# U's products clear their bank with a product of zeros, and batch 1's first stage is placed behind layer 1's first products

## The chip, the cores and the metric

The kernel runs on one core of one Trainium2 chip. The metric is the device time of one execution in microseconds; a kernel's time is the median of its runs.

## What is computed

The reference, cut to what matters (x is 8 batches of 3136 rows by 256 columns; all values are float32):

```python
def _attn_ref(x, w_r, w_i, b_r, b_i):
    X = np.fft.rfft(x, axis=1)
    Yr = X.real @ w_r - X.imag @ w_i + b_r
    Yi = X.real @ w_i + X.imag @ w_r + b_i
    lam = 0.01
    Yr = np.sign(Yr) * np.maximum(np.abs(Yr) - lam, 0.0)
    Yi = np.sign(Yi) * np.maximum(np.abs(Yi) - lam, 0.0)
    return np.fft.irfft(Yr + 1j * Yi, n=x.shape[1], axis=1)

def _moe_ref(x, U, V, w_ch1, w_ch2):
    xt = x.transpose(0, 2, 1)
    h = xt @ U @ V                     # U: 3136 x 32, V: 32 x 3136
    u = x + h.transpose(0, 2, 1)
    ch = np.maximum(u @ w_ch1, 0.0) @ w_ch2      # 256 -> 1024 -> 256
    return u + ch
```

The output is the second function applied to the first.

## The kernel before

Each batch goes through two transforms and then two dense layers. The transform of 3136 points is split into one of 49 and one of 64 points. The stages carry the names of their PSUM tiles (a PSUM tile fills one bank of 512 floats per partition):

- `psa` (`a_mm`): the first stage of the forward transform, eight groups c = 0 to 7 a batch. One group is 24 matmuls; ScalarE (ACT) copies one bank out, VectorE (DVE) makes a sum and a difference of the two (into the tiles `xt`), and four transfers, issued by SyncE (SP), store them to memory (`gd`).
- `psb`, `psy`, `psc`: the second forward stage, the product with the complex weights and the shrinking, and the first inverse stage. Batch 0's results go through 32 x 32 transposes on DVE (`zz` from `t0t`).
- `psd` (`d_unit`): the second inverse stage. Its right operand `du` has 81 columns for each frequency: 49 for output points, and 32 more that hold the transform's matrix times U, so that the same matmul gives the projection on U. The stage has six units of two halves each. Every half fills two banks, which ACT copies into `xq` and from which DVE adds 32 columns into `pa`.
- `psu` (`make_ud`): once in the program, the matmuls that fill these 32 columns of `du`, for six groups of frequencies (6, 6, 4, 6, 6 and 4 of them). Each frequency takes four small matmuls, into four bands of partitions of one bank (25, 24, 25 and 24 rows). ACT then copies the four bands out, one operation each, so a group takes four copies, 24 in all. The two banks (`psm0`, `psm1`) that the six groups take in turn also serve the first pair of `psd`.
- `p_spread`, `p_unit`: `pa` is spread by DVE into `pr`, turned by TensorE (`psp`) and written into the tile `w1x`.
- `u_prep`: `psv`, the product with V, is added to `xq` by DVE; from the sum come the operands `oa`, `ob` and `od` (high and low parts, `oah`, `oal` and so on).
- `psy`, `psx`, `psz` and then `pso`: layer 1 in seven half-sized products for each pair of chunks, and layer 2. The tiles `s`, `v`, `rh` and `rl` lie between the two.
- Weights arrive as 64-bit words and are decoded on DVE and ACT (`dm`, `dp`, `dl`, `wa`, `w2t`, `w1x`).
- `setup_w` computes `wt` and `wis`, from which ACT and GpSimd (POOL) make the mixing weights `wmt` of the batches from 1 on.

The program is recorded as a list of operations and ordered by a planner, `_Program.order`, with an estimated cost of each. It runs list passes forward and backward over the operations and their dependences. In the code as written, the place of an operation decides how early it is wanted and who gets a free buffer first. Where TensorE would be idle in the plan, the planner puts fills at line 561: products of an identity, 128 columns each, into a bank that is free (`idle<-ident`); a fill leaves two records in the trace. Nearly all other operations are issued from line 563, so the profile's rows say L563 and are told apart by their tiles.

Batch 0's whole transform comes first. Batch 1's first stage is loaded from line 1648 on. Its groups 0 and 1 are called at line 1658, and groups 2 to 7 on a side list (line 2000) that runs along with the first dense chunks, with positions 2 + 2(c - 2).

Of the kernel before, what the change touches and what calls it, by code (L numbers as in the profile page):

```python
# [29 lines left out]
R = 32  # L30
# [14 lines left out]
K1 = 49  # L45
KP = 56
C81 = K1 + R
# [524 lines left out]
def fft_mix_moe_kernel(  # L572
# [58 lines left out]
    def acopy(o, i):  # L631
        return act.activation(o, i, AF.Copy)
# [137 lines left out]
    def a_mm(b, c, loads=()):  # L770
        xt = a_state.pop((b, c))
        ps = banks(0, f"psa_{b}_{c}")

        def products():

            def mm(j, q, e, o, l, r):
                pe.matmul(
                    ps[j][32 * q : 32 * q + 32, o : o + r.ids[0].size],
                    lhsT=fq[64 * j : 64 * j + K1, l : l + 32],
                    rhs=r,  # L780
                    start=True,
                    stop=True,
                    tile_position=(64 * j, 32 * q),
                    skip_group_check=True,
                )

            for i in range(2):
                for q in range(4):
                    cc, e = divmod(q, 2)
                    if i == 0:  # L790
                        mm(0, q, e, 0, 32 * cc, xt[e][0:K1])
                    own = 64 if (c, e, i) == (0, 0, 0) else 0
                    mm(1, q, e, D * i, own + 32 * cc, xt[1 - e][64 : 64 + K1, 1 - i])

        first = in_group(products)
        first.preds.update((e.n, e) for e in loads)
        p0, p1 = [p.rearrange("p (i d) -> p i d", i=2) for p in ps]
        even, odd = xt
        acopy(odd, p1)
        dve.tensor_tensor(out=even, in0=p0, in1=odd, op=ALU.add)  # L800
        if c == 0:
            for cc in range(2):
                q = slice(64 * cc, 64 * cc + 32)
                acopy(even[q, 0], p0[q, 0])
            lo = odd[:, 1]
            dve.tensor_tensor(out=lo, in0=p0[:, 1], in1=lo, op=ALU.subtract)
            for cc in range(2):
                q = slice(64 * cc + 32, 64 * cc + 64)
                dve.tensor_tensor(out=odd[q, 0], in0=p0[q, 0], in1=odd[q, 0], op=ALU.subtract)
        else:  # L810
            dve.tensor_tensor(out=odd, in0=p0, in1=odd, op=ALU.subtract)
        g = gd[b % 2].rearrange("e k a (s c i) d -> c s a (e k) (i d)", s=2, i=2)
        for cc in range(2):
            at = slice(64 * cc, 64 * cc + 64)
            dma.dma_start(g[c, 0, cc], even[at])
            dma.dma_start(g[c, 1, 1 - cc], odd[at])
# [662 lines left out]
    def load_fdt(c):  # L1479
        dma.dma_start(fdt[:, 8 * c : 8 * c + 8], c_fdt[:, 8 * c : 8 * c + 8, :])  # L1480

    def make_ud(t):
        n0, n = UNITS_D[t]
        ps = psm([128, 512], f"psu_{t}", 2)
        parts = [(64 * j + 32 * r, K1 * j + 25 * r, 25 - r) for j in range(2) for r in range(2)]
        for k in range(n):
            for p, c, m in parts:
                mm = pe.matmul(
                    ps[p : p + m, R * k : R * k + R],
                    lhsT=fdt[:, n0 + k, c : c + m],  # L1490
                    rhs=us[:, n0 + k, :],
                    start=k == 0,
                    stop=k == n - 1,
                    tile_position=(0, p),
                    skip_group_check=True,
                )
                if t > 0:
                    mm.preds[prog.idlers[2].n] = prog.idlers[2]
        for p, _, m in parts:
            p = slice(p, p + m)  # L1500
            u = du[t][p, 0 : n * C81].rearrange("p (q c) -> p q c", c=2 * C81)
            acopy(u[:, :, K1 : K1 + 2 * R], ps[p, 0 : R * n].rearrange("p (q r) -> p q r", r=2 * R))

    def load_v(c):
        load_words(vw[:, 392 * c : 392 * c + 392], (128, 392), ("v", c, 0))
# [103 lines left out]
    def on(n, f, *args):  # L1609
        first.append((n, lambda: f(*args)))  # L1610
# [35 lines left out]
    loads = []  # L1646
# [8 lines left out]

    for c in range(4):
        on(129 + c / 10, load, c)
    on(133, lambda: [a_mm(1, c, loads if c == 0 else ()) for c in range(2)])
    loads1 = []
    for c in range(4):  # L1660
        on(129.5 + c / 10, load, 4 + c, loads1)
# [308 lines left out]
    n = len(prog.ops)  # L1970
# [5 lines left out]
    side = []  # L1976
# [9 lines left out]
    for w, prev, next_w in zip(turn_w, [None] + turn_w, turn_w[1:] + [None]):  # L1986
        b, j = divmod(w, NW)
        if j == 0 and b < NB:
            assert not side
            side = [(6.5, lambda b=b: rest_unit(b))]  # L1990
            if b + 1 < NB:
                start, mid, end = (1, 58, 84) if b else (START, 71, 86)

                side += bmc_spread(b + 1, start, mid - 6)
                if b + 2 < NB:
                    at = four_at(b + 1, start, mid - 6)
                    some = (0, 1, 1, 2, 3, 3, 4, 5) if shared(b + 1) else (0, 1, 2, 2, 3, 4, 4, 5)
                    side += a_spread(b + 2, [at[k] for k in some])
                if b == 0:
                    side += [(2 + 2.0 * (c - 2), lambda c=c: a_mm(1, c, loads1 if c == 4 else loads if c == 0 else ())) for c in range(2, 8)]  # L2000
                    side += [(8 + t, lambda t=t: keep_du(t)) for t in (3, 4, 0, 1, 2)]
                    side += [(32, lambda: dma.dma_start(vd[2:4], vd[0:2]))]
                    side += [(34 + k, lambda k=k: pad_z(1 - k)) for k in range(2)]
                side += d_spread(b + 1, mid - 4, end)
                side += [(end + 0.5, lambda b=b: p_spread(b + 1)), (end + 1.5, lambda b=b: p_unit(b + 1))]
            else:
                side += [(40, rest_load)]
            side.sort(key=lambda z: z[0])
        for g in range(2):
            l1s = l1_chunks(w, g)  # L2010
            new = l2_chunks(w, g)
            for k in range(4):
                for c in range(2):
                    n = WS * j + 8 * g + 2 * k + c
                    if c == 0:
                        l1s[k]()
                    elif l2s:
                        l2s.pop(0)()
                    s = 8 * g + 2 * k + c
                    if s == 1 and next_w not in (LAST, None):  # L2020
                        v_load(next_w)
                    if s == 9 and prev is not None:
                        out_unit(prev)
                    if next_w is not None:
                        if s == 9:
                            up = u_prep(next_w)
                        if s >= 10:
                            up[s - 10]()
                    while side and side[0][0] <= n:
                        side.pop(0)[1]()  # L2030
            l2s = new
# [119 lines left out]
```

## Time and profile before

| what | us |
|---|---|
| median of 3 runs | 1577.74 (1576.67 to 1577.82) |
| profiled execution | 1575.85 |
| its span, first to last instruction | 1574.1 |
| TensorE matmuls (PE) busy | 1546.7 |
| VectorE (DVE) busy | 1294.2 |
| ScalarE (ACT) busy | 926.1 |
| GpSimd (POOL) busy | 421.4 |

PE and PEld are TensorE's matmuls and its weight loads, which run beside the matmuls. "issue" in the chain of waits is time in which an engine waited for nothing that the profile shows. The granted clock (PEclk) is a share of full speed: 1.00 is 2.4 GHz and 0.50 is 1.2 GHz. The queue called "instruction" in the table of transfers carries the engines' own instructions.

### The profile page before, as it was taken

The page shows a single profiled execution, that of the slowest core. Times are in us where ns is not written, and L with a number is a line of the kernel's source. Part 1 is how long each engine was busy: PE and PEld are TensorE (multiplying, and loading weights), DVE is VectorE, ACT ScalarE, POOL GpSimd, SP SyncE. Part 2 cuts the span into 40 slices and gives each one's busy share as a digit, 9 for nine tenths or more (in the row PEclk, how much of TensorE's full clock was granted, in tenths as well). Part 3 has the DMA queues.
Part 4 walks back from the last instruction along what each step waited for, and adds up shares of the span by engine and source line. Part 5 has one row for each costly group of instructions (what it writes and reads, how often), then busy time and mean ns, then how long its engine had stood idle before and what let it go on. Part 6 is the DMA issues. An engine that isn't in the chain of part 4 may idle for free.

```text
span 1574.1 us, 43271 instructions
## 1 busy us (share of the span) xinstructions
PE 1546.7 (98%) x17604; PEld 1392.4 (88%) x17604; DVE 1294.2 (82%) x2351; ACT 926.1 (59%) x1756; POOL 421.4 (27%) x366
## 2 busy tenths in 40 slices
PE   9978999999999999999999999999999999999998
PEld 6966889988898899998898889989898998999997
DVE  5979899689977899779986899778996789866775
ACT  3876565556655666556655666555665565555553
POOL 1311233123322333213331233222232133312221
PEclk9999999999999999999999999999999999999999
DMA  6665566636764465535665465644565025520332
GB/s 159 181 164 126 157 197 160 162 101 160 185 155 112 111 177 135 145 87 143 153 149 137 121 165 134 151 112 112 143 161 144 25 85 123 120 81 8 83 65 37
DMA packets 227309, 201.64 MB, mean 128 GB/s; under 512 B 131127, under 2 KB 191018, under 8 KB 227030
## 3 DMA queue, kind: packets, MB, share of 16 engines
q1 hardware_dynamic: 224472, 198.01, 49.7%
q8 instruction: 139, 2.28, 0.6%
q10 hardware_dynamic: 2638, 0.86, 0.3%
q14 instruction: 60, 0.49, 0.1%
HBM read 118.54 MB, written 82.27 MB: 128 GB/s over the span
## 4 chain that ended last, share of the span: by engine, by line
PE 91%; DVE 4%; DMA 1%; issue 1%; ACT 1%; SPq 1%; POOL 0%; DVEq 0%; POOLq 0%; ACTq 0%
PE pso L563 32%; PE psy L563 18%; PE psx L563 8%; PE psq L563 7%; PE psd L563 6%; PE psa L563 4%; PE psz L563 4%; PE psc L563 4%; PE pst L563 3%; PE psb L563 3%; PE psv L563 1%; PE idle L561 1%; SPq L563 1%; DMA xx<-in_x_dram 1%; DVE ys L563 1%
## 5 line engine op out<-in xcount | busy, mean ns | idle before, releaser
L563 PE MATMUL pso<-rh,w2t 128*128 128x512 f32 x1568 | 407.1, 382 | 0.5 <-issue 0.5
L563 PEld LDWEIGHTS pso<-rh,w2t 128*128 128x128 f32 x1568 | 273.4, 190 | 32.8 <-issue 4.8
L563 PE MATMUL pso<-rl,w2t 128*128 128x512 f32 x784 | 233.6, 379 | 0.4 <-DVE rl L563 0.4
L563 POOL TENSOR_TENSOR yl<-ys,yh 128x512 fp32r<-128x512 f32 x88 | 114.0, 1295 | 250.9 <-ACT yh L563 155.7
L563 ACT ACTIVATE rh<-s 128x512 fp32r<-128x512 f32 x196 | 121.8, 627 | 86.1 <-DVE s L563 81.2
L563 PEld LDWEIGHTS pso<-rl,w2t 128*128 128x128 f32 x784 | 148.0, 189 | 21.9 <-DVE rl L563 1.0
L563 DVE SCALAR_TENSOR_TENSOR rl<-s,rh 128x512 fp32r<-128x512 f32 x196 | 151.5, 777 | 17.1 <-ACT rh L563 15.2
L563 DVE SCALAR_TENSOR_TENSOR ys<-tb,rl 64x256 f32<-64x256 f32 x350 | 156.0, 446 | 9.5 <-ACT rl L563 4.1
L563 PE MATMUL psy<-odh,w1x 128*128 128x256 f32 x784 | 122.1, 278 | 0.9 <-DVE s L563 0.9
L563 PE MATMUL psq<-wmt,xsh 128*128 128x256 f32 (+1 forms) x704 | 122.5, 275 | 0.0
L563 PEld LDWEIGHTS psy<-odh,w1x 128*128 128x128 f32 x784 | 110.7, 192 | 10.3 <-DVE s L563 1.1
L563 POOL TENSOR_TENSOR w1x<-xq,w1x 128x256 fp32r<-128x256 f32 x48 | 35.9, 747 | 299.9 <-DVE tt L563 110.3
L563 PEld LDWEIGHTS psq<-wmt,xsh 128*128 128x128 f32 (+1 forms) x704 | 109.6, 191 | 3.0 <-DVE s L563 0.4
L563 POOL TENSOR_TENSOR tl<-ts,th 128x512 fp32r<-128x512 f32 (+2 forms) x46 | 56.6, 1231 | 183.0 <-ACT th L563 124.3
L563 POOL TENSOR_TENSOR odl<-tt,odh 128x512 fp32r<-128x512 f32 x49 | 63.7, 1301 | 154.5 <-ACT odh L563 92.4
L563 ACT ACTIVATE xq<-psd 128x294 f32<-128x294 f32 (+1 forms) x192 | 69.9, 444 | 52.9 <-PE psd L563 51.8
L563 PE MATMUL psq<-wmt,xsl 128*128 128x256 f32 (+1 forms) x352 | 96.8, 275 | 0.0
L563 DVE SCALAR_TENSOR_TENSOR rl<-psy,rh 128x512 fp32r<-128x512 f32 x98 | 66.9, 683 | 30.7 <-ACT rh L563 29.9
L563 ACT ACTIVATE rl<-tb,lam 128x512 f32<-128x512 f32 x88 | 63.6, 723 | 46.8 <-DVE tb L563 46.5
L563 ACT ACTIVATE s<-psy 128x512 f32<-128x512 f32 x98 | 58.5, 597 | 53.1 <-PE psy L563 49.3
L563 ACT ACTIVATE s<-psx 128x512 f32<-128x512 f32 x98 | 58.2, 594 | 53.4 <-PE psx L563 52.1
L563 ACT ACTIVATE rh<-v 128x512 fp32r<-128x512 f32 x98 | 61.6, 628 | 47.1 <-DVE v L563 46.4
(211 smaller groups left out, 3891.0 us busy)
## 6 DMA issues: line engine op xcount, KB each, us to landing
gd<-xt SPq DMA_DIRECT2D x224, 128.0 KB
zt<-zd SPq DMA_DIRECT2D x112, 224.0 KB
out_dram<-os SPq DMA_DIRECT2D x190, 128.0 KB
t<-gd SPq DMA_DIRECT2D x168, 128.0 KB
zd<-zs SPq DMA_DIRECT2D x84, 256.0 KB
xt<-in_x_dram SPq DMA_DIRECT2D x88, 224.0 KB
vw<-vd SPq DMA_DIRECT2D x44, 256.0 KB
fb<-in_fb_dram SPq DMA_DIRECT2D x54, 128.0 KB
```

The source lines that it names most:

```text
L561: engines["pe"].matmul(o[:, 0:128], lhsT=junk, rhs=junk, start=True, stop=True)
L563: made = call(*[real(a) for a in op.args], **{k: real(a) for k, a in op.kw.items()})
```

## The change

The six groups of `psu` get one more matmul each, ahead of the others: a 128 x 128 block of zeros times 128 or 192 columns of zeros, which starts the bank (`start=True`) on all 128 partitions. The small matmuls then all add to it. With the whole bank written, ACT copies all 128 partitions in one operation. The zeros are the second half of `wt`, which holds them until `setup_w` writes it. At line 1658 no group of batch 1's first stage is called any more; the side list has all eight, at positions 3 + 2c.

```diff
+    zero = wt[:, 1]
+
     def make_ud(t):
...
+        pe.matmul(
+            ps[:, 0 : R * n], lhsT=zero[:, 0:128], rhs=zero[:, 0 : R * n], start=True, stop=False, skip_group_check=True
+        )
         for k in range(n):
             for p, c, m in parts:
                 mm = pe.matmul(
...
-                    start=k == 0,
+                    start=False,
...
-        for p, _, m in parts:
-            p = slice(p, p + m)
-            u = du[t][p, 0 : n * C81].rearrange("p (q c) -> p q c", c=2 * C81)
-            acopy(u[:, :, K1 : K1 + 2 * R], ps[p, 0 : R * n].rearrange("p (q r) -> p q r", r=2 * R))
+        u = du[t][:, 0 : n * C81].rearrange("p (q c) -> p q c", c=2 * C81)
+        acopy(u[:, :, K1 : K1 + 2 * R], ps[:, 0 : R * n].rearrange("p (q r) -> p q r", r=2 * R))
...
-    on(133, lambda: [a_mm(1, c, loads if c == 0 else ()) for c in range(2)])
+    on(133, lambda: [a_mm(1, c, loads if c == 0 else ()) for c in range(0)])
...
-                    side += [(2 + 2.0 * (c - 2), lambda c=c: a_mm(1, c, loads1 if c == 4 else loads if c == 0 else ())) for c in range(2, 8)]
+                    side += [(3 + 2 * (c - 0), lambda c=c: a_mm(1, c, loads1 if c == 4 else loads if c == 0 else ())) for c in range(0, 8)]
```

What the planner makes of it is seen at three places. The first is ScalarE between batch 0's last `psc` and its first `psd`. The number behind a tile's name tells tiles of one kind apart; `25x3x64` is 25 partitions of three times 64 columns. Before:

```order
L563 ACTIVATE t0t<-psc_12_1044 128x2x256
L563 ACTIVATE du_745<-psu_1067 25x3x64
L563 ACTIVATE du_745<-psu_1067 24x3x64
L563 ACTIVATE du_745<-psu_1067 25x3x64
L563 ACTIVATE du_745<-psu_1067 24x3x64
L563 ACTIVATE du_859<-psu_1097 25x2x64
...
L563 ACTIVATE du_880<-psu_1201 24x2x64
...
L563 ACTIVATE xq_0_1274<-psd_1_0_0_1234 128x294
```

Of the change:

```order
L563 ACTIVATE t0t<-psc_12_1053 128x2x256
L563 ACTIVATE dm_1094<-dw_924 128x512
L563 ACTIVATE du_745<-psu_1075 128x3x64
L563 ACTIVATE du_853<-psu_1110 128x2x64
L563 ACTIVATE du_966<-psu_1133 128x3x64
L563 ACTIVATE du_966<-psu_1163 128x3x64
L563 ACTIVATE du_863<-psu_1194 128x2x64
L563 ACTIVATE dm_1215<-dw_1010 128x512 x2
L563 ACTIVATE xq_0_1264<-psd_0_0_0_1231 128x294
```

Five groups have five copies where they had twenty, two decoding operations (`dm`) stand nearer, and the first unit of `psd` is unit 0 where it was unit 1.

The second place is TensorE from the end of `psd` to layer 1's first products. `psa_2_1` is the second bank of group 2; "x5" are rows that read alike. Before:

```order
L563 MATMUL psd_5_1_1_1586<-du_880,zz_1283 64x81
L561 MATMUL idle<-ident 128x128 x5
...
L563 MATMUL psa_0_1_1624<-xt_0_0_981,fq 32x256 x5
L561 MATMUL idle<-ident 128x128 x3
...
L563 MATMUL psa_1_1_1657<-xt_1_0_1010,fq 32x256 x5
L563 MATMUL psp_1673<-ident,pr_1630 128x128 x2
L561 MATMUL idle<-ident 128x128 x9
L563 MATMUL psv_0_1703<-vw_1196,w1x 128x512
...
L563 MATMUL psa_2_1_1719<-xt_2_0_1029,fq 32x256 x5
...
L563 MATMUL psa_3_1_1752<-xt_3_0_1070,fq 32x256 x5
L561 MATMUL idle<-ident 128x128 x5
L563 MATMUL psy_0_1785<-obh_1744,w1x 128x256 x4
```

Of the change:

```order
L563 MATMUL psd_5_1_1_1581<-du_863,zz_1275 64x81
L561 MATMUL idle<-ident 128x128 x14
L563 MATMUL psp_1641<-ident,pr_1616 128x128 x2
L561 MATMUL idle<-ident 128x128 x4
...
L563 MATMUL psa_0_1_1659<-xt_0_0_982,fq 32x256 x5
L563 MATMUL psv_0_1673<-vw_1069,w1x 128x512
L563 MATMUL psv_1_1677<-vw_1069,w1x 128x512
L561 MATMUL idle<-ident 128x128 x3
...
L563 MATMUL psa_1_1_1689<-xt_1_0_1017,fq 32x256 x5
L561 MATMUL idle<-ident 128x128 x8
L563 MATMUL psy_0_1730<-obh_1701,w1x 128x256 x4
...
L563 MATMUL psa_2_1_1744<-xt_2_0_1046,fq 32x256 x5
```

Two groups of batch 1 stand ahead of layer 1's first product where there were four, `psp` stands ahead of both of them, and the fills number 29 where they were 27.

The third place is VectorE from `psp`'s copy to `obl`, the last operand of layer 1's first product. Before:

```order
L563 TENSOR_TENSOR w1x<-psp_1673,w1x 64x256
L563 TENSOR_TENSOR xt_0_0_981<-psa_0_0_1621,xt_0_0_981 128x512
L563 TENSOR_TENSOR xt_1_0_1010<-psa_1_0_1654,xt_1_0_1010 128x512 x2
L563 TENSOR_TENSOR xq_0_1274<-xq_0_1274,psv_0_1703 128x16x32
L563 SCALAR_TENSOR_TENSOR dm_1649<-dw_1124,dm_1649 128x512
L563 TENSOR_TENSOR xq_0_1274<-xq_0_1274,psv_1_1708 128x16x32
...
L563 TENSOR_TENSOR xt_2_0_1029<-psa_2_0_1717,xt_2_0_1029 128x512
L563 TENSOR_TENSOR obl_1769<-xq_0_1274,obh_1744 128x512
```

Of the change:

```order
L563 TENSOR_TENSOR w1x<-psp_1641,w1x 64x256
L563 TENSOR_SCALAR dp_1651<-dm_1094 128x512
L563 TENSOR_TENSOR dp_1651<-dl_1614,dp_1651 128x512
L563 TENSOR_TENSOR dm_1094<-dm_1094,w2t 128x512
L563 TENSOR_TENSOR w2t<-dm_1094,dp_1651 128x512
L563 TENSOR_TENSOR xq_0_1264<-xq_0_1264,psv_0_1673 128x16x32
L563 TENSOR_TENSOR xq_0_1264<-xq_0_1264,psv_1_1677 128x16x32
...
L563 TENSOR_TENSOR xt_0_0_982<-psa_0_0_1657,xt_0_0_982 128x512
L563 TENSOR_TENSOR obl_1710<-xq_0_1264,obh_1701 128x512
L563 TENSOR_TENSOR xt_1_0_1017<-psa_1_0_1687,xt_1_0_1017 128x512 x2
```

Of the sums of `psa`, one stands ahead of `obl` where there were four; between `psp`'s copy and the sums with `psv` there now lie four decoding operations.

Besides, `setup_w`'s two operations on DVE, which stood at 73.5 and 85.5 us, are placed behind layer 1's first chunks (the zeros are read until then), and with them the copies and differences that make `wmt`; SP's loads stand in nearly the same order, with one `dw` load earlier and the `vraw` loads together.

## Rows read from the trace of the kernel before

**Rows 1.** The page: engines' busy times, and the instruction queue's packets, MB, share.

```profile
PE 1546.7 (98%) x17604; PEld 1392.4 (88%) x17604; DVE 1294.2 (82%) x2351; ACT 926.1 (59%) x1756; POOL 421.4 (27%) x366
...
q8 instruction: 139, 2.28, 0.6%
```

**Rows 2.** Stretches: length, busy time and count by engine, clock, DMA share, GB/s.

```profile
81.00:97.50 16.50, 13.39 (x324) 10.90 (x322) 14.72 (x25) 14.52 (x37) 5.73 (x5) 1.00 0.85 226
97.50:117.00 19.50, 13.96 (x523) 12.60 (x524) 12.97 (x37) 11.08 (x31) 0.00 (x0) 0.91 0.50 131
117.00:129.00 12.00, 12.00 (x155) 8.77 (x153) 11.43 (x23) 9.79 (x22) 2.52 (x2) 1.00 0.24 57
129.00:143.00 14.00, 10.48 (x102) 8.15 (x101) 13.33 (x25) 6.86 (x13) 1.94 (x2) 0.88 0.62 156
143.00:160.00 17.00, 15.88 (x133) 12.84 (x132) 16.45 (x30) 9.03 (x17) 3.09 (x3) 1.00 0.62 148
160.00:1566.40 1406.40, 1403.83 (x15846) 1271.65 (x15845) 1165.79 (x2124) 826.11 (x1542) 386.17 (x323) 1.00 0.50 125
```

**Rows 3.** The same stretches, line 561 (fills) alone: PE, PEld.

```profile
81.00:97.50 16.50, 7.03 (x52) 6.26 (x52) 1.00 0.85 226
...
117.00:129.00 12.00, 6.83 (x54) 6.17 (x52) 1.00 0.24 57
```

**Rows 4.** Timeline of ACT: start, length, operation, count.

```profile
90.81 6.37 ACT L563 ACTIVATE du<-psu 25x192 f32<-25x192 f32 x20
```

**Rows 5.** Chain of waits that ends in 145 us: start, length, what.

```profile
96.72 0.84 issue
...
100.36 0.94 issue
...
104.64 3.04 issue
107.67 2.18 PE psd L563 x57
109.85 0.72 PE idle L561 x2
110.57 4.15 PE psd L563 x197
114.72 1.50 issue
116.22 0.50 PE psd L563 x11
```

**Rows 6.** Transfers from 104.4 to 107.7 us: queue, packets, MB, share.

```profile
q8 instruction: 1, 0.02, 2.5%
```

**Rows 7.** Timeline of SP's issuing: start, length, transfer, count.

```profile
98.49 5.24 SPq L563 DMA_DIRECT2D xt<-in_x_dram  x10
```

**Rows 8.** Timeline of DVE from the transposes to layer 1.

```profile
90.94 9.02 DVE L563 STREAM_TRANSPOSE zz<-t0t 128x512 f32<-128x512 f32 x15 [0.48 <-ACT t0t L563]
...
117.87 0.42 DVE L563 TENSOR_TENSOR pr<-pa 128x256 f32<-128x256 f32 x1
...
127.74 0.68 DVE L563 TENSOR_TENSOR obl<-xq,obh 128x512 fp32r<-128x512 f32 x1
...
129.74 2.91 DVE L563 TENSOR_TENSOR xt<-psa,xt 128x512 f32<-128x512 f32 x5
...
137.34 0.68 DVE L563 TENSOR_TENSOR s<-psz,s 128x512 f32<-128x512 f32 x1
```

**Rows 9.** Timeline of PE around layer 1's first products.

```profile
123.10 0.68 PE L563 MATMUL psv<-vw,w1x 128*128 128x512 f32 x2
...
130.73 1.09 PE L563 MATMUL psa<-xt,fq 49*32 49x512 f32 x24
...
138.07 0.98 PE L563 MATMUL psx<-oah,w1x 128*128 128x256 f32 x4 [1.82 <-DVE s L563]
...
140.69 1.59 PE L563 MATMUL psa<-xt,fq 49*32 49x512 f32 x24
```

## The prediction

> **What bounds the kernel now.** I read the page first: TensorE is busy for 1546.7 of 1574.1 us [rows 1], so only time in which it does no useful work can be won. The table of stretches says where that is. From 160 us on, 1403.83 of 1406.40 us are busy, and from 117 to 129 us all 12.00 [rows 2]; but half of the latter are fills, 6.83 us [rows 3]. The change neither adds nor takes away useful matmuls except six small ones. So what counts is the ramp from batch 0's last mix (81 us) to layer 1 (about 143 us), and I read it in three parts.
>
> In 81 to 97.5 us, where `psu` is, TensorE has 13.39 us of work, 7.03 of them fills; ScalarE is busy 14.52 of 16.5 us, VectorE 14.72 [rows 2, 3]. ScalarE's twenty small copies alone take 6.37 us in a row, and VectorE's transposes end at 99.96 us, at 0.60 us each (9.02 us for 15) [rows 4, 8].
>
> In 97.5 to 117 us, where `psd` is, no engine is full: TensorE has 13.96 of 19.5 us [rows 2]. The chain of waits shows waits named "issue", in which TensorE waits for nothing that the profile shows: 0.84, 0.94, 3.04 and 1.50 us, 6.3 together [rows 5]. Between the third and the fourth lie 57 + 2 + 197 = 256 matmuls [rows 5], with their weight loads 512 instructions. The page has 139 packets of instructions, 16.4 KB each; TensorE's 35208 instructions are 253 a packet [rows 1]. In the third wait one such packet moves [rows 6], while SP has just issued ten loads of `xt` (98.49 to 103.73 us) [rows 7]. I read these waits as TensorE running out of instructions: `psd` has small, short matmuls and reaches the end of a piece before the next has come. `psd` ends at T = 116.72 us [rows 5].
>
> From T to 143 us it is VectorE. From the end of `pr` (118.29 us) to the end of `s` (138.02 us) it works without a gap worth naming, 19.7 us, and TensorE stands 1.82 us for that `s` [rows 8, 9]. At the end of this part the clock is low: 0.88 over 129 to 143 us [rows 2], so 0.12 x 14.0 = 1.7 us of work are lost in a stretch at the half level (1.2 GHz), which begins behind that wait; the same group of `psa` takes 1.59 us there and 1.09 us before [rows 9].
>
> **The change, part by part.** Profiled execution 1575.85 us, 1.89 below the median of 1577.74; I sum against the first and add 1.89.
>
> (1) Copies and zero products, up to T. Twenty ScalarE copies become five (the sixth lies earlier and is alike). The trace has no copy of 128 partitions by 192 columns. It costs no less than one of 25 partitions, 6.37 / 20 = 0.32 us [rows 4], and no more than an operation on 128 x 512, 0.68 us [rows 8]; so five cost 1.6 to 3.4 us, and 3.0 to 4.8 us of ScalarE are freed. Two decoding copies that stand there in the new order take back up to 2 x 0.68 = 1.4, which leaves at least 1.6. The six zero products cost TensorE, at a fill's 6.83 / 27 = 0.25 us for 128 columns [rows 3] (two records a fill), 4 x 0.38 + 2 x 0.25 = 2.0 us. They lie where TensorE has 7.03 us of fills and 3.1 us of nothing [rows 2, 3], so I price them at 0; with no cover, the one ahead of the last copy is on the path, 0.4 us.
>
> What reaches T is not what ScalarE frees. `psd` starts when `du`, the first transposes and its instructions are there. It waited 0.84 us for the latter at its start and 5.5 us within [rows 5]. If each piece is asked for only after the last boundary is crossed, and takes as long as before, an earlier ScalarE brings the first boundary forward and no more. Counting the new order, TensorE has 28 more instructions ahead of `psd`, so the boundary that fell two matmuls into `psd` now falls into the nine fills ahead of it, with six fills behind, 1.5 us by [rows 3]. Ends: 0 (the pieces eat it) and -3.0 (all that ScalarE surely frees before the two decoding copies). The copies are bounded from rows and the pieces only inferred, so neither end is nearer; I take the middle, **-1.5**.
>
> (2) VectorE from `pr` to `s`. The order has 31 operations there where there were 35. Of nine sums of `psa`, four are gone, which are the row of five (2.91 us) less one at 0.60, so -2.3 [rows 8]. A sum of `xq` with `psv` comes in, +0.60; decoding is one operation and some 0.15 us shorter, as more of it waits for the operation just before. Together **-1.9**; -1.5 of it lies before `obl` (15 operations for 18, less 0.3 for waits on the one before), -0.4 after. It all counts while VectorE has no gap there. What is late next is TensorE's own row: between `psy` and `s` it gets one `psa` (1.09) and two `psv` (0.68) more [rows 9], 1.8 us, and had 14.00 - 10.48 = 3.5 us to spare there [rows 2], so VectorE stays last. The ends are -0.4 (TensorE late from `psp` on) and -2.6 (no operation waits for the one before). `psp` ahead of both `psa` only helps it.
>
> (3) Moved products. One group of `psa` less is done when the first second-chunk `psx` starts, +1.09 us [rows 9], and two `psv` more, -0.68 [rows 9]: **+0.4** (0 to +1.1). They come later into time that is full.
>
> (4) The half-clock stretch. It began behind waits for VectorE and cost 1.7 us [rows 2]. The waits shrink, since the 1.8 us of added work fill half of the 3.5 us. Whether that spares the stretch the trace doesn't tell: 0 to -1.7, middle **-0.8**.
>
> (5) `setup_w` behind layer 1's first chunks: its two operations of VectorE, 2 x 0.60 by [rows 8], leave a full stretch and enter another, where VectorE is busy 16.45 of 17.00 us but TensorE 15.88 [rows 2]. Its readers are batch 1's mixing products, which come after 160 us. 0, with +1.2 if VectorE is the bound there. SP's queue has its loads in nearly the old order; the ten `xt` loads come up to 3 us earlier, as their place follows `psu`, and with them the crowding of the transfers; that is rival A.
>
> Sum: -1.5 - 1.9 + 0.4 - 0.8 = -3.8, so 1575.85 - 3.8 = 1572.05 profiled, and **1573.9** as a median.
>
> **The rivals.**
>
> A: the pieces keep the pace. Each piece comes a fixed time after the boundary before, and `psd` gains nothing from the copies; the burst of `xt` loads slows a packet as it did in the 3.04 us wait [rows 5, 7]. For it: 6.3 us of waits, spaced as above. Against: the first boundary lies inside `psu`, and comes sooner with fewer copies. T moves by 0 and the clock's stretch stays: -1.9 + 0.4 = -1.5, 1576.2. At worst six fills stand between the piece and `psd`: T + 1.5, moved products at +1.1: +0.7, 1578.4.
>
> B, on the other side: VectorE becomes the bound of layer 1's first 30 us. Behind `obl` it now has three sums of `psa` (1.8 us) and `wt` and `wis` (1.2), 3.0 us more, in stretches where it has 0.7 and 0.6 us free [rows 2]. TensorE then waits for `s` and `rl` in pieces, and two more stretches at the half level of 1.7 us each would follow: 1575.85 - 1.5 + 3.0 + 3.4 = 1580.75, 1582.6. It decides if TensorE waits more than some 3.5 us from 143 to 160 us (before: 17.00 - 15.88 = 1.1). Against: the moved sums free banks that nobody in these stretches waits for.
>
> C: the "issue" waits are not the pieces' and go along with whatever moves. T then moves by the whole 3.0, the smoother start spares the clock's stretch: -3.0 - 1.9 + 0.4 - 1.7 = -6.2, 1571.5. Against it stands the spacing of 256. The Trainium skill, "Runtime: NRT & Kernel Launch", section "Instruction fetch mechanics", says that instructions are refilled in blocks of 256 by the sequencer while the current block runs, and that crossing a block is "mostly hidden". The trace agrees with the size of 256 and disagrees with "hidden" in `psd`: 6.3 us of waits stand at the crossings [rows 5]. By the rule the result would be C's 1571.5.
>
> That the change doesn't do what it says is unlikely: the order shows six copies and two groups ahead of layer 1.
>
> **How the numbers follow.** A measurement of this kernel can tell 0.2%, 3.15 us, from no change: faster is below 1574.6, slower above 1580.9. The forecast has 0.50 (its own range, from the middle terms being off by half, is 1572.2 to 1575.8; two thirds of it lie below 1574.6); A 0.25, C 0.15, B 0.10. Faster 0.32 + 0.15 = 0.47, same 0.18 + 0.25 = 0.43, slower 0.10. The range goes from C with the moved products at 0, -6.6, 1571.1, to A at its worst, 1578.4, and leaves B out.
>
> **What would show it.** (1) Six `du` copies of at most 0.68 us; `psd` ends near 115.2; if T stays near 116.7 with the waits as large as before, A. The waits should still lie 256 instructions apart, the first in fills ahead of `psd`; if they are gone, C. (2) `obl` ends about 10.2 us behind T (before 11.7), `s` about 19.4 (before 21.3), VectorE without gaps between. (3) One `psa` less before the `psx` behind `s`. (4) The clock over the 14 us behind `psy`: 0.88 or nearer 1. (5) TensorE's waits from 143 to 160 us near 1.1. The forecast is wrong if time moves after 160 us, where I expect none.

## The result and the profile after

The changed kernel is slower: a median of 1584.5 us (1583.72 to 1589.57) where the forecast was 1573.9 and its range ended at 1578.4. The ratio to the kernel before, measured beside it, is 1.0053, with an interval of 1.0039 to 1.0067. Here and below the ratio is taken from all runs of a series; the two medians alone would give 1.0043.

| what | before | after |
|---|---|---|
| median, us | 1577.74 | 1584.5 |
| profiled execution, us | 1575.85 | 1583.72 |
| its span, us | 1574.1 | 1581.6 |

The page of the changed kernel, busy times and the instruction queue, to be laid beside [rows 1]:

```profile
PE 1556.1 (98%) x17620; PEld 1399.9 (89%) x17620; DVE 1295.3 (82%) x2351; ACT 917.4 (58%) x1738; POOL 423.6 (27%) x366
...
q8 instruction: 139, 2.28, 0.6%
```

ScalarE has lost 8.7 us of work, and TensorE is busy 9.4 us longer with 16 more matmuls. A product at the half clock is busy twice as long (four of `pso` take 2.07 us and 1.04 in the rows below), so the table of stretches has to tell where this time is. Its columns are as in [rows 2]; the stretch behind 160 us is cut further:

```profile
81.00:97.50 16.50, 15.30 (x341) 12.68 (x340) 16.09 (x26) 9.74 (x20) 6.43 (x5) 1.00 0.77 210
97.50:117.00 19.50, 16.49 (x538) 15.30 (x538) 13.49 (x41) 12.54 (x34) 0.00 (x0) 0.82 0.50 128
117.00:129.00 12.00, 12.00 (x129) 8.31 (x128) 11.70 (x22) 6.43 (x14) 0.69 (x1) 1.00 0.18 45
129.00:143.00 14.00, 12.95 (x136) 10.08 (x136) 13.70 (x28) 7.62 (x14) 1.76 (x2) 1.00 0.61 140
143.00:160.00 17.00, 15.92 (x160) 12.23 (x151) 16.86 (x29) 10.76 (x21) 5.15 (x5) 1.00 0.77 176
160.00:175.00 15.00, 10.78 (x109) 9.61 (x108) 8.09 (x16) 5.45 (x10) 2.55 (x2) 0.77 0.77 181
230.00:1060.00 830.00, 827.18 (x9905) 745.20 (x9903) 690.31 (x1279) 492.48 (x931) 231.49 (x191) 1.00 0.55 141
```

The kernel before, in the last two of these stretches:

```profile
160.00:175.00 15.00, 15.00 (x169) 12.49 (x169) 12.04 (x24) 8.53 (x16) 2.55 (x2) 1.00 0.65 170
...
230.00:1060.00 830.00, 829.77 (x10010) 747.20 (x10010) 695.07 (x1292) 497.43 (x941) 233.67 (x195) 1.00 0.55 141
```

From 160 to 175 us TensorE now stands still for 4.22 us, and the clock's mean is 0.77, which loses another 0.23 x 15.0 = 3.4 us of work: 7.7 us in a stretch where before was full. What it waits for shows in TensorE's timeline of the changed kernel, from its last products ahead of the place to the next at full speed:

```profile
161.54 0.39 PE L563 MATMUL psx<-oal,w1x 128*128 128x256 f32 x2
...
165.17 0.30 PE L563 MATMUL psb<-fb,t 64*64 64x64 f32 x2 [3.24 <-DMA t<-gd]
166.44 1.98 PE L563 MATMUL psb<-fb,t 64*64 64x64 f32 x62 [0.98 <-DMA t<-gd]
168.35 2.07 PE L563 MATMUL pso<-rh,w2t 128*128 128x512 f32 x4
...
172.35 1.04 PE L563 MATMUL pso<-rh,w2t 128*128 128x512 f32 x4
```

The same first `psb` in the kernel before:

```profile
168.62 1.16 PE L563 MATMUL psb<-fb,t 64*64 64x64 f32 x64
```

It is batch 1's second forward stage, and it waits for `t`, the load from memory of what batch 1's first stage had stored there. Before, the first `psb` came 7.0 us behind the first of these loads and waited for nothing. Now TensorE is there at 161.9 us, 3.3 us behind the first load, and the data are not. SP's issuing says when the loads went out; of the changed kernel, the stores (`gd`) of batch 1's last groups, two loads that spread the biases `b_r` and `b_i` over all partitions (`bias`), and the loads of `t`:

```profile
145.52 11.26 SPq L563 DMA_DIRECT2D gd<-xt  x16
156.82 0.60 SPq L563 DMA_DIRECT2D bias<-in_b_r_dram  x1
157.46 0.44 SPq L563 DMA_DIRECT2D bias<-in_b_i_dram  x1
158.67 1.76 SPq L563 DMA_DIRECT2D t<-gd  x4
160.47 2.69 SPq L563 DMA_DIRECT2D xt<-in_x_dram  x4
```

and of the kernel before:

```profile
153.98 1.84 SPq L563 DMA_DIRECT2D bias<-in_b_r_dram  x1
155.87 0.43 SPq L563 DMA_DIRECT2D bias<-in_b_i_dram  x1
156.39 2.37 SPq L563 DMA_DIRECT2D gd<-xt  x4
161.60 1.77 SPq L563 DMA_DIRECT2D t<-gd  x4
163.41 1.70 SPq L563 DMA_DIRECT2D xt<-in_x_dram  x4
```

The loads go out 2.9 us earlier than before, but TensorE asks 6.7 us earlier (161.9 against 168.6). Of that, 3.5 us are the ramp's gain, and 3.2 us come from the order: TensorE's row has so much less work ahead of the first `psb` than in the kernel before.

Laid beside each other by the same amount of useful TensorE work done, the two traces differ as follows (after less before; the last is the difference of the spans):

| at | us |
|---|---|
| end of `psd` | -1.5 |
| just ahead of the first `psb`, about 161 us | -3.5 |
| behind the first `psb` | +4.5 |
| 175 to 230 us | +3.5 |
| 330 us | +4.1 |
| end | +7.5 |

So in this trace the ramp was won (how much of that was luck is told below), twice as much was lost at one place that the prediction did not look at, and some 4 us more were lost in many small pieces behind it.

### The profile page after: what moved, and what is told of

Same layout as the page of the kernel before. It is cut to its first block, busy times and chain, and to the rows that moved or that the text cites. A ratio compares the mean times of both kernels' runs of the same rounds, so it can differ in the third digit from the quotient of the medians.

```text
span 1581.6 us, 43327 instructions
## 1 busy us (share of the span) xinstructions
PE 1556.1 (98%) x17620; PEld 1399.9 (89%) x17620; DVE 1295.3 (82%) x2351; ACT 917.4 (58%) x1738; POOL 423.6 (27%) x366
## 4 chain that ended last, share of the span: by engine, by line
PE 49%; DVE 7%; issue 1%; DMA 1%; SPq 1%; ACT 0%; DVEq 0%; ACTq 0%
PE pso L563 19%; PE psy L563 10%; PE psx L563 5%; PE psd L563 3%; PE psq L563 3%; PE psz L563 2%; DVE ys L563 2%; PE psc L563 1%; PE psa L563 1%; PE pst L563 1%; PE psb L563 1%; DVE tb L563 1%; DVE rl L563 1%; DVE os L563 1%; SPq L563 1%
## 5 line engine op out<-in xcount | busy, mean ns | idle before, releaser
L563 POOL TENSOR_TENSOR obl<-xq,obh 128x512 fp32r<-128x512 f32 x47 | 61.2, 1301 | 137.0 <-ACT oah L563 45.6
```

The lines of the kernel that those rows point to most:

```text
L563: made = call(*[real(a) for a in op.args], **{k: real(a) for k, a in op.kw.items()})
```

## The experiments

All times are medians with the ratio to the kernel before as measured in the same series. One kernel's runs scatter: 17 runs of the kernel before went from 1574.38 to 1579.81 us, so a ratio's interval is about 0.1% to either side, and a trace is one execution of these. Differences inside a trace are told by equal work, as in the table above.

### Which part of the change: U's products alone, and the move alone

U's products alone (lines 1658 and 2000 as before). In the diff, the part of the change that is made:

```diff
+        pe.matmul(
+            ps[:, 0 : R * n], lhsT=zero[:, 0:128], rhs=zero[:, 0 : R * n], start=True, stop=False, skip_group_check=True
+        )
...
-                    start=k == 0,
+                    start=False,
```

> The kernel before with the U part alone (zero products, one copy a group); batch 1's groups stay where they were. Theory (the loss is TensorE standing 4.2 us for the loads of t, batch 1's second-stage operand, and a half-clock stretch behind it, both brought by the moved groups): no wait at the first psb of more than 0.3 us, psd ends 1 to 2 us earlier, time 1574.5 to 1577.5. Rival (the U part itself, by 28 more instructions or by the moved setup_w, costs the time): 1580 or more, with the loss ahead of 160 us.

Measured: 1579.58, ratio 1.0018 (1.0006 to 1.0030). By equal work it is 1.4 us ahead from 175 to 210 us and 1.2 behind at the end. The time lies between the theory's and the rival's, and `psd` ends at 117.1 us and not earlier; but its first `psb` doesn't wait, as the theory said:

```profile
164.96 1.16 PE L563 MATMUL psb<-fb,t 64*64 64x64 f32 x64
```

The move alone:

```diff
-    on(133, lambda: [a_mm(1, c, loads if c == 0 else ()) for c in range(2)])
+    on(133, lambda: [a_mm(1, c, loads if c == 0 else ()) for c in range(0)])
...
-                    side += [(2 + 2.0 * (c - 2), lambda c=c: a_mm(1, c, loads1 if c == 4 else loads if c == 0 else ())) for c in range(2, 8)]
+                    side += [(3 + 2 * (c - 0), lambda c=c: a_mm(1, c, loads1 if c == 4 else loads if c == 0 else ())) for c in range(0, 8)]
```

> The kernel before with the move of batch 1's groups alone; 24 copies and no zero products. Theory: VectorE's row from pr to s is shorter by some 2 us, and TensorE stands 2 us or more for t<-gd at the first psb of batch 1, with half-clock behind it: 1579 to 1584. Rival (U part is to blame): 1576 or less, no wait there.

Measured: 1584.22, ratio 1.0045 (1.0031 to 1.0059), nearly the whole change's, and within 0.3 us of the theory's range. TensorE's waits in it (engine, line and what it waited for: total us, times, the longest):

```profile
PE psd L563 <- issue: 8.4, 5, 2.5
PE psb L563 <- DMA t<-gd: 3.6, 2, 2.6
```

Behind that wait 6.8 us at the half clock follow, and by equal work it is 4.9 us behind the kernel before at 175 us. So the wait at the first `psb` belongs to the move.

### What the wait at the first psb is: four ways around it

Rivals here: the load is slow because the next batch's loads share the transfers with it; `psb` merely stands too early in TensorE's row, and other ready work could fill the wait; or the whole of batch 1's first stage comes too late for it.

First, the changed kernel with the four loads of `xt`, which follow the loads of `t`, put behind the next `t` loads in SP's row:

```diff
+        if q.eng == "sp" and named(q) in ("xt_2_1_0", "xt_2_2_0"):
+            q.start += 8.0
```

> The changed kernel with one difference in SP's row: the four loads of batch 2's xt (224 KB each), which are issued right behind the four loads t<-gd, stand behind the next four of these. All other orders are as they were. If the loads of t are late because they share the transfer engines with the xt loads (engines 99% busy from 162 to 166 us): data 2 us or more earlier, wait at psb 2 us or less instead of 4.2, time 1579 to 1582, or 1577 if the half-clock stretch goes as well. If they are late by their own latency and the stores before them: wait still about 4, time 1583 to 1585.

Measured: 1583.38, ratio 1.0038 (1.0024 to 1.0053). The wait is 1.2 us shorter and the half clock behind it lasts 3.4 us instead of 6.8:

```profile
PE psb L563 <- DMA t<-gd: 3.0, 2, 2.3
```

Sharing explains 1.2 of 4.2 us in these two traces, not the rest; the wait lies between the two expectations, and the time is that of loads late by themselves.

Second, the changed kernel with twelve products of layer 2 that stand behind the first `psb` put ahead of it:

```diff
+    ahead = [q for q in prog.ops if q.eng == "pe" and P < q.start < P + 4.5 and named(q).startswith("pso_0_")]
+    for k, q in enumerate(sorted(ahead, key=lambda q: q.start)):
+        q.start = P - 0.01 + 0.0001 * k
```

> The changed kernel with one difference in TensorE's row: twelve pso products (2.6 us of work) that stood behind the first psb of batch 1 stand ahead of it. Theory (TensorE comes to psb too early): the wait is 4.2 - 2.6 = 1.6 us, time 1581 to 1582.5, and about 1578.5 if the half-clock stretch goes with it. Rival (the order of the rest of the program makes the loss, and the wait would be made up later): 1584 or more, unchanged.

Measured: 1584.49, ratio 1.0047 (1.0032 to 1.0063). The wait shrinks as expected, the clock doesn't fall there, and one new wait comes behind it (`psv`):

```profile
PE psb L563 <- DMA t<-gd: 1.6, 2, 1.1
...
PE psv L563 <- DVE xsl L563: 1.0, 1, 1.0
```

At 180 us it is 3.1 us behind the kernel before, against 3.5 us of the changed kernel, and 7.6 at the end. But in this trace `psd` ended at 117.0 us and not at 115.2, with the same order up to there. From 161 to 175 us, across the place, it loses 3.9 us by equal work where the changed kernel loses 7.0. So some 3 us are saved at the place, and the later end of `psd` hides them. The median doesn't show the saving: it is the rival's, and why is not shown.

Third, the groups called earlier on the side list:

```diff
-                    side += [(3 + 2 * (c - 0), lambda c=c: a_mm(1, c, loads1 if c == 4 else loads if c == 0 else ())) for c in range(0, 8)]
+                    side += [(1 + 0.5 * c, lambda c=c: a_mm(1, c, loads1 if c == 4 else loads if c == 0 else ())) for c in range(0, 8)]
```

> The changed kernel, with batch 1's groups at positions 1 + 0.5c on the side list instead of 3 + 2c. In TensorE's row the first psb stands some 16 us of work behind the last group, where the changed kernel has some 12 and the kernel before 13. Theory (the moved groups' stores and loads come too late for psb): no wait over 0.5 us at that psb, no half-clock stretch behind it, ahead of the kernel before by 1 to 4 us at 170 us; time 1575 to 1581, according to the later order. Rival (the wait has another cause than the groups' place): wait of 3 to 4 us again, 1583 or more.

Measured: 1582.15, ratio 1.0031 (1.0018 to 1.0043). The first `psb` no longer waits for `t`, but `psd` ends at 120.6 us where the changed kernel has 115.2, and by equal work 3.1 us are lost at 175 us all the same, earlier in the ramp. There `psv` now waits 1.4 us for `vw`, another load, which stands among the stores. The time is above the theory's range. The same kernel was run once more, with nothing held, to see whether that end of `psd` is its own:

> A second look at the changed kernel with the groups at 1 + 0.5c, as it was run before: in its first profile psd ended 3.9 us later than in the kernel before, with the same matmuls. If the waits at the instruction pieces change from run to run, psd ends 2 us or more earlier this time; if they belong to the order, it ends within 1 us of 120 us again.

Measured: one run of 1582.1; `psd` ends at 119.3, and the first `psb` waits 0.5 us. So in two traces this end belongs to the order, within 1.3 us. The waits up to it (excess over the step between two instructions) were 2.0, 2.2 and 2.1 us the first time and 1.3, 3.8 and 0.9 the second: 6.3 and 6.0 us in sum, in other parts, the first two at the same instructions.

Last, the changed kernel with a planner that is told that these four loads take 4 us longer than it assumed:

```diff
-                    dma.dma_start(t[p : p + 32, k : k + m], src)
+                    got = dma.dma_start(t[p : p + 32, k : k + m], src)
+                    if (b, q) == (1, 0):
+                        got.lag += 4.0
```

> The changed kernel, with one number of the planner changed: the four loads of t for batch 1's first psb are taken to land 4.0 us later than the planner takes them to (in the changed kernel they were some 3 to 4 us later than planned). The planner then puts the groups ahead and psb later. Theory: no wait at psb, ramp slower than the changed kernel's as VectorE has the groups' sums ahead of layer 1 again; time 1576 to 1582. Rival (loads come late wherever they stand): wait of 2 us or more, 1583 or more.

Measured: 1581.4, ratio 1.0036 (1.0023 to 1.0050). No wait at `psb`, but the planner now puts all of batch 1's groups ahead of layer 1's second products; `obl` ends 16.6 us behind `psd` (11.0 in the changed kernel) and `s` 25.8 (20.3). What was a wait at `psb` has become VectorE's row ahead of layer 1, as the theory said. The profiled execution is the slowest of this kernel's nine (1587.84 us), so its rows may be worse than those of the median. None of the four ways gets back to the kernel before.

When TensorE reached the first `psb`, and when all of its data were there, in us behind the issue of the first `t` load (from the traces' timelines of PE and SP); how long ahead of that load the second `bias` load was issued; and from when to when the packets of the four `t` loads ran. Both kinds of load have packets of 1 KB; taken in order, the first 256 are the two `bias` loads and the next 512 are `t` (the other way round in the kernel told of late loads):

| kernel | TensorE there | data there | `bias` ahead by | packets of `t` |
|---|---|---|---|---|
| before | 7.0 | by 7.0 | 5.7 | 1.0 to 3.3 |
| U's products alone | 5.6 | by 5.6 | 6.2 | 1.0 to 3.3 |
| whole change | 3.3 | 7.8 | 1.2 | 2.8 to 6.7 |
| move alone | 4.6 | 8.5 | 0.7 | 3.3 to 7.6 |
| change, `xt` loads later | 3.5 | 6.8 | 1.2 | 2.8 to 5.8 |
| change, layer 2 first | 6.2 | 8.2 | 1.2 | 2.5 to 6.7 |
| change, groups earlier | 9.5 | by 9.5 | 1.4 | 3.7 to 8.9 |
| change, planner told | 4.4 | by 4.4 | `bias` behind | 0.5 to 2.7 |

So the `bias` loads are a part of the wait that none of the four ways aims at. Where they stand right ahead, the packets of `t` begin only as theirs end; where they stand some 6 us ahead, `t` is done in 3.3 us. They are slow, too: 256 KB take 3.4 us in the kernel before and 3.6 in the changed kernel, where the 512 KB of `t` take 2.3 and 3.9. The changed kernel's transfers before and after `t`'s packets begin (the columns are as in [rows 2], GB/s the last):

```profile
158.70:161.40 2.70, 2.70 (x21) 2.54 (x20) 2.64 (x5) 1.88 (x3) 1.41 (x2) 1.00 0.74 74
161.40:165.20 3.80, 0.56 (x6) 0.40 (x6) 3.03 (x6) 1.23 (x2) 0.29 (x1) 1.00 1.02 238
```

The kernel whose planner was told has them behind, and its `psb` finds its data there 4.4 us behind the issue:

```profile
155.17 1.76 SPq L563 DMA_DIRECT2D t<-gd  x4
156.97 0.44 SPq L563 DMA_DIRECT2D bias<-in_b_r_dram  x1
157.45 0.43 SPq L563 DMA_DIRECT2D bias<-in_b_i_dram  x1
```

Of the 3.4 us by which `t`'s last packet ends later in the changed kernel than before, 1.8 are thus the later begin and 1.6 the slower transfer. No kernel was run with the `bias` loads alone moved, so what that would save is not shown.

The planner's own figure for such a load is 2.6 us and the time to move it, some 3.1 us in all. In its plan of the changed kernel the last of the loads lands 1.3 us ahead of `psb`; in that of the kernel before, 4.6 us ahead, and this slack covered what the figure lacks.

### The rest of the program: noise, and the old order held fast

The kernel before with a little noise added to the planner's starts from 190 us on (two seeds), and nothing else:

```diff
-CHANGES = ()
+CHANGES = ((1, 1.0, 190.0, 2000.0),)
```

> The kernel before, with noise of 1 us (one seed) on the planner's lateness of all operations that are wanted behind 190 us. The order up to there is the old one row for row; behind it the same work stands in another order. Theory (after 200 us the changed kernel loses some 4 us because its later order is another one, and not by anything that the change does there): the start as before, a loss of 1 to 6 us spread behind 200 us, time 1577.5 to 1582.5. Rival (the later order is of no matter, and the 4 us are the change's own): 1576 to 1577.5.

> The same with another seed, to see how far two such orders lie apart. Theory: also 1 to 6 us over the kernel before, and 1 us or more apart from the first seed. Rival: both within 1 us of the kernel before.

Measured: 1584.33, ratio 1.0046 (1.0035 to 1.0058), and 1582.62, ratio 1.0042 (1.0030 to 1.0054). At 200 us the two lie within 0.1 and 0.6 us of the kernel before; at the end they are 5.9 and 6.1 us behind, by the difference of the spans. That is the theory's, and for the first seed more than its range. With seed 1, from 230 to 1060 us:

```profile
230.00:1060.00 830.00, 826.64 (x9879) 743.97 (x9883) 694.34 (x1284) 493.37 (x935) 231.09 (x194) 1.00 0.55 139
```

TensorE is idle for 3.4 us there. The kernel before has 0.2 in this stretch and the changed kernel 2.8. Both orders are worse than the one that the planner found for the kernel before; two seeds don't tell how rare such an order is.

So the three kernels of interest were run again with the old order held: first the kernel before is planned, and every operation that starts there at 200 us or later keeps its place in the row.

```diff
+            body = [PINS[k][1] if k in PINS and PINS[k][1] >= PIN_FROM else None for k in keys]
...
+            place = self.strict(units, tags, [t if v is None else v + off for v, t in zip(body, starts)])
```

The whole change, pinned:

> The changed kernel up to about 200 us of the plan, row for row; behind that, all engines' rows in the order of the kernel before (on TensorE its last 7518 of 8596 rows, word for word). Theory (half of the loss is the later order, the rest the wait at psb): the profile behind 220 us loses nothing against the kernel before, and what it is behind at 210 us in the changed kernel (3.5 us) stays: 1578.5 to 1581.5. Rival (what comes late in the start goes on costing behind 200 us): 1583.5 to 1585.5 as the changed kernel.

Measured: 1583.39, ratio 1.0037 (1.0024 to 1.0050), within 0.2 us of the rival's range and far from the theory's. The wait is there with the old order behind it (line 634 is line 563 in this kernel):

```profile
168.66 0.29 PE L634 MATMUL psb<-fb,t 64*64 64x64 f32 x2 [1.96 <-DMA t<-gd]
169.97 1.69 PE L634 MATMUL psb<-fb,t 64*64 64x64 f32 x62 [1.02 <-DMA t<-gd]
```

Here `psd` ended at 119.2 us, 4.0 us later than in the changed kernel, and `psb` starts when it did in the kernel before. It waits all the same: stores and loads move with the ramp (TensorE is there 4.1 us behind the first load), and what decides is the distance between the loads and `psb` in the order, and what stands in the queue ahead of them, not the clock time.

U's products, pinned:

> The U part alone up to about 200 us, and behind it the order of the kernel before. The run with the U part alone was 1.4 us ahead at 210 us and 1.2 us behind at the end. Theory: 1.4 us ahead to the end: 1574 to 1576.5, ahead of both kernels. Rival: the lead is lost again, 1577.5 to 1580.

Measured: 1578.04, ratio 1.0005 (0.9995 to 1.0014): no difference, and the rival's range. In its trace the 0.9 us won by 210 us are gone again behind 310 us, where `psd` of a later batch waits at the end of a piece of instructions (+1.1); the rest of the program ends 1.0 us behind.

The move, pinned:

> The move of batch 1's groups alone up to about 200 us, and behind it the order of the kernel before. The run with the move alone was 4.9 us behind at 210 us and 9.8 at the end. Theory: 4.9 us behind to the end: 1579.5 to 1582.5. Rival: 1584 to 1586 as the move alone.

Measured: 1584.17, ratio 1.0044 (1.0032 to 1.0056), as without the pin, so the rival's again. By equal work it is 4.8 us behind at 175 us; 2.4 more come from 215 to 235 us, where some rows still stand in a new order, and the end is at +9.5.

## Why the prediction was wrong

**The step that failed** is the one on the moved products, (3), with the sentence "They come later into time that is full", and behind it "I expect none" on time after 160 us. It priced the moved groups as TensorE's time and VectorE's sums and stopped there. The groups are stored to memory and loaded again, and the first `psb` is the reader of the last of them. The prediction asked for `setup_w` who its readers were, and did not ask it for the groups. And in (5) it took SP's queue to have "its loads in nearly the old order": the two `bias` loads, 5.7 us ahead of `t`'s before, now stand 1.2 us ahead of them. The cost is the 4.2 us wait and 3.4 us of work lost to the clock behind it, 7.7 us by the table of stretches, where before had nothing. The experiments show that it belongs to the move (there with the move alone and in both pinned kernels with the move, absent with U's products alone, pinned or not) and that 1.2 us of the wait are the sharing of transfers. For the other 3.0 us the traces show TensorE coming 3.7 us sooner behind the loads (3.3 against 7.0) and the packets of `t` beginning 1.8 us later, behind those of `bias`; no run takes the two apart.

**The second miss** is that the order of everything behind 160 us was taken as given. The changed kernel lost 4.0 us between 175 us and the end. That another order alone can cost this much is shown: two kernels that compute and place the same up to 190 us and differ by noise behind lost 6 us. That it is what the changed kernel lost is not shown. With the old order held, its trace still loses 2.7 us from 175 us on (U's products alone 1.9 where they lost 2.6, the move alone 4.7 where it lost 4.9). From 230 to 1060 us TensorE is idle for 1.8 to 1.9 us in the three, where the kernel before has 0.2. The ratio goes from 1.0053 to 1.0037 for the change, and from 1.0018 to 1.0005 for U's products; the intervals overlap, so the size of this share stays open.

**(1) U's products.** The copies cost what the lower bound said. ScalarE's timeline of the changed kernel:

```profile
84.55 0.34 ACT L563 ACTIVATE du<-psu 128x192 f32<-128x192 f32 x1
91.95 0.48 ACT L563 ACTIVATE du<-psu 128x192 f32<-128x192 f32 x2
93.50 0.34 ACT L563 ACTIVATE du<-psu 128x192 f32<-128x192 f32 x1 [1.07 <-PE psu L563]
94.57 0.33 ACT L563 ACTIVATE du<-psu 128x192 f32<-128x192 f32 x1 [0.73 <-PE psu L563]
95.40 0.28 ACT L563 ACTIVATE du<-psu 128x128 f32<-128x128 f32 x1 [0.49 <-PE psu L563]
```

That is some 0.3 us each, 0.48 + 0.34 + 0.33 + 0.28 = 1.43 us for the last five, where twenty took 6.37 [rows 4]. `psd` ended at 115.17 us, where 115.2 was forecast, but that was luck. Three more kernels with the same order up to there ended it at 115.8, 117.0 and 119.2 us; the mean of the four is 116.8. The kernel before and the two with noise behind have 116.7, 116.3 and 117.3, mean 116.8. With U's products alone it ended at 117.1 us, pinned or not. So in these few traces the copies gain nothing at `psd`'s end on average, as rival A said of this term, and the waits up to that end, which change from trace to trace, set it. In the changed kernel these two stand inside it (in brackets the wait, and that the profile shows nothing else that was waited for):

```profile
105.14 0.81 PE L563 MATMUL psd<-du,zz 56*64 56x81 f32 x13 [2.74 <-issue]
...
114.52 0.65 PE L563 MATMUL psd<-du,zz 56*64 56x81 f32 x21 [0.27 <-issue]
```

and in the pinned one, in the same order of work, they are larger, one of them in the fills ahead of `psd`:

```profile
98.87 2.50 PE L632 MATMUL idle<-ident 128*128 128x128 f32 x11 [2.65 <-issue]
...
109.90 0.81 PE L634 MATMUL psd<-du,zz 56*64 56x81 f32 x13 [3.28 <-issue]
```

Rival C fell: in every kernel run here the waits stand 256 instructions apart or a multiple of it, and take 3.3 to 9.1 us together. The Trainium skill, "Runtime: NRT & Kernel Launch", section "Instruction fetch mechanics", calls the cost of crossing a block of instructions "mostly hidden"; around `psd` these traces disagree.

**(2) VectorE** held. From the end of `pr` to the end of `s` it took 19.7 us before [rows 8]; in the changed kernel:

```profile
116.96 0.43 DVE L563 TENSOR_TENSOR pr<-pa 128x256 f32<-128x256 f32 x1
...
125.52 0.68 DVE L563 TENSOR_TENSOR obl<-xq,obh 128x512 fp32r<-128x512 f32 x1
...
134.83 0.68 DVE L563 TENSOR_TENSOR s<-psz,s 128x512 f32<-128x512 f32 x1
```

18.1 us, so -1.6 where -1.9 was forecast, and 18.1 in each of the three other kernels with this order. But `pr` ends 2.2 us behind `psd`, where it was 1.6 before: an earlier `psd` finds VectorE still at decoding and sums. From `psd`'s end to `s` the gain is 1.0 us, 0.2 to 1.4 over the four.

**(4) The clock.** The stretch from 129 to 143 us went from 0.88 [rows 2] to 1.00, and the wait for `s` to 0.76 us:

```profile
135.56 0.71 PE L563 MATMUL psx<-oah,w1x 128*128 128x256 f32 x4 [0.76 <-DVE s L563]
```

So this term was -1.7, its far end, where -0.8 was taken. `psd`'s stretch went from 0.91 [rows 2] to 0.82, which loses 0.09 x 19.5 = 1.8 us more there; that loss is part of where `psd` ended.

**The ramp together** came out at -3.5 us at 161 us, where the sum said -3.8, and in part that was luck as well. The three other traces with the same order up to there have -3.3, -0.9 and +1.2 us, so the mean of the four is -1.6 us. It comes from behind `psd`'s end, where the four gain 1.2 to 2.4 us. **Rival B** gave 1582.6, nearest to the result, and did not happen: TensorE waits 17.00 - 15.92 = 1.1 us from 143 to 160 us, as before, and the time was lost after that. The case on the slow side had the right size and the wrong place, and 0.10 was too little for it.

**What stays open.** In the pinned kernels 1.6 to 4.4 us are still lost behind 200 us; 2.4 of the most, those of the move, lie where some rows stand in a new order. With U's products, 1.1 lie at the end of a piece of instructions that falls elsewhere; the rest is spread over waits below 1 us. Each kernel has one trace, or two, while its runs scatter by some 3 to 9 us. No kernel run here beats the kernel before; U's products with the old order held are level with it.

## What to carry to other kernels

Follow what is moved to the last reader of its results, through stores, loads and queues, and see what stands ahead of a load in its queue: a transfer's slack in the order can be worth more than all the work that is saved ahead of it, and time that looks full has no room for a wait. Where a planner makes the order, an edit can make all of it anew: measure by a little noise what the present order is worth, and hold the rest of it when one part is tried, though here that did not bring the loss back. A gain in front of a stage that runs out of instructions may not arrive behind it, so look at such a stage in more than one trace.

## What the runs showed of the hardware

- The waits named "issue" lie at fixed counts of TensorE's instructions, matmuls and weight loads together: 193 more than a multiple of 256, in all kernels, however the programs differ ahead of them. Around the first `psd`, with its small matmuls, one takes up to 3.8 us, and the same instruction in the same kernel waited 2.2 us once and 3.8 the other time. Behind 200 us few show, of 0.3 to 1.8 us, nearly all in a later `psd`.
- Loads of 128 KB, four in a row, were there 6.8 to 8.6 us behind the first one's issue in the six kernels whose first `psb` waited 1.6 us or more, with two slow loads (`bias`, 256 KB in some 3.6 us) just ahead in the queue, and by 4.4 us where these stood behind. The transfer engines were the more loaded in the changed kernel; the busy share in the 4.3 us behind that issue, of the changed kernel:

```profile
q1 hardware_dynamic: 646, 0.60, 85.1%
```

and of the kernel before, in 4.4 us:

```profile
q1 hardware_dynamic: 647, 0.77, 71.4%
```

  More share for fewer bytes (0.60 MB against 0.77), as the packets of `bias` run in the first.
- The granted clock fell to its half level (1.2 GHz) behind the two waits at the first `psb`: for 6.8 us behind 3.2 + 1.0 us and behind 2.7 + 1.0 us, for 3.4 us behind 2.3 + 0.7 us and, in the pinned kernels with the move, behind 2.0 + 1.0 and 2.3 + 1.2 us; behind 0.6 + 1.1 us it did not fall. So such a wait cost here up to 3.4 us of work more than its own length.
- A copy on ScalarE from a bank costs the same for 128 partitions as for 25: 0.34 us for 128 x 192, and 0.32 for 25 x 192 [rows 4].
